# A Fourier mixing block whose loads of the next batch's x are held behind other transfers, and whose sums for the mixing come later

## The chip, the cores and the metric

One NeuronCore of a Trainium2 chip runs the whole program. The metric is device time in microseconds (us), the median of three runs.

## The reference

Two stages on x of shape (8 batches, 3136 positions, 256 channels). The first is a convolution by Fourier transform along the positions; the second adds a two-dimensional transform's real part, normalizes each row, and applies a two-layer product.

```
X = rfft(x, axis=1);  Y = X * (filt_r + 1j*filt_i);  y = irfft(Y, n=3136, axis=1)
mixed = real(fft(fft(y, axis=1), axis=2))
u = y + mixed;  un = (u - mean(u)) / sqrt(var(u) + 1e-6)        # per row of 256
out = u + relu(un @ w_ch1) @ w_ch2                              # 256 -> 1024 -> 256
```

## The kernel before

**Stages of one batch.** The transforms are written as matrix products in two stages each. `forward1` loads x of a batch in seven pieces of 448 KB (`x<-x`), takes the largest magnitude of each piece on VectorE (`absmax`, tile `mx`), makes a scale from all seven (TensorE transposes `pt_x` and spreads `pb_x`), and multiplies by s1 in 14 steps (`s<-x,s`); each step's result goes to DRAM (`d<-ast`). `forward2` loads it back in seven chunks (`at<-d`), multiplies by s2 (`s<-s,at`), applies the filter on VectorE and GpSimd (`yt`), and turns the result by a DMA transpose (`z<-y`). In `fold` GpSimd forms the sums and differences (`ef`, `eo`) that the mixing needs, in a ring of 1920 slots. `inverse1` multiplies z (`i<-z,i`, two products a chunk) and stores to DRAM (`d<-bt`). `inverse2` loads that back in seven pieces of 448 KB (`b<-d`), multiplies by i2 (`y<-b,i`, 14 products a batch) and stores rows to DRAM (`dy<-ys`).

**Groups.** The second part works on 49 groups of 256 slots (6.125 groups a batch). `fetch` loads a group's rows (`y<-dy`); `prepare` mixes (`mix`), normalizes and transposes by DMA (`ut<-u`); `first_product` (`h<-ut,w1s`, 48 matmuls a group) and `second_product` (`acc<-w2s,h`, 96 a group) follow, and `out<-y` stores. Each h is read by ScalarE and then by VectorE (line 746), into two PSUM buffers in turn.

**What sets the order.** Python generators are advanced step by step in the main loop over q, eight q a group: `advance` moves the forward stages (STEPS = 59 steps a batch), `give` the second inverse stage (BACK steps a batch). A scheduler then orders each engine's instructions by its own timeline; `after(key)` puts an instruction behind the marked one on the same engine. The first product of `inverse2` and of `forward2` of a batch stand behind the last h matmul traced. Every DMA is issued from one queue, SP, in order. The pool `xp` has seven buffers of one size for x, at and z together; `b` has two.

Of the kernel before, what the change touches and what calls it, by code (L numbers as in the profile page):

```python
# [25 lines left out]
NS = N // 2  # L26
# [11 lines left out]
BACK = 15  # L38
EARLY = 0.5
RISE = 28  # L40
SOON = 930
LOAD_AT = (15, 16, 17, 18, 19, 27, 28, 25)
# [3 lines left out]
BOUND_AT = (63, 76)  # L46
SPLIT_AT = (63, 101)
# [143 lines left out]
def _program(ctx, tc, nc, a, NB):  # L191
# [166 lines left out]
    def forward1(b, d1):  # L358
# [3 lines left out]
        for q in range(7 + lag):  # L362
            with after(("y", 0), ("un", 0)) if b == 1 else nullcontext():
                if q < 7:
                    nc.sync.dma_start(xs[q], a["x"][b, :, 4 * q : 4 * q + 4])
# [33 lines left out]
    def forward2(b, d1, d2):  # L399
# [108 lines left out]
        for c in range(9):  # L508
            work = [
                (c, spectrum, 0), (c, spectrum, 1), (c, fold, None), (c - 2, inverse1, 0), (c - 2, inverse1, 1),  # L510
# [7 lines left out]
    def inverse2(b, d2):  # L518
# [6 lines left out]
        def load(c):  # L525
            if c < 7:
                bts[c] = fp.tile([112, 4, 2, 256], F16, tag="b2", name=f"b2_{b}_{c}", bufs=2)
                with after("dy"):
                    nc.sync.dma_start(bts[c].rearrange("p j h c -> p (j h) c"), d2v[:, 8 * c : 8 * c + 8])

        def store(k, s, r, ys, c, j0):
            rows = dy[k, 224 * c : 224 * c + 224].rearrange("(j s q) c -> s q j c", j=4, s=2)
            marks["dy"] = nc.sync.dma_start(rows[s, :, j0], ys[r : r + 28, j0]).ins

        load(0)
        yield
# [113 lines left out]
    def prepare(g):  # L650
# [52 lines left out]
        for t, (g0, g1) in enumerate(tiles):  # L703
# [10 lines left out]
            marks["ut", g] = nc.sync.dma_start_transpose(ut[:, t, :, :m], u16[:m].rearrange("p k d l q -> p (k d l q)")).ins  # L714
# [36 lines left out]
    def second_product(g, f):  # L751
# [8 lines left out]
        for t, (g0, g1) in enumerate(tiles):  # L760
# [12 lines left out]
            if f == 7:  # L773
# [3 lines left out]
                marks["out", g] = nc.sync.dma_start(a["out"][:, g0:g1].rearrange("k s c -> s k c"), y[:m, t]).ins  # L777
# [96 lines left out]
    def give(n):  # L874

        while come[0] < min(n, NB * BACK) and done[0] >= STEPS * (come[0] // BACK + 1):
# [59 lines left out]
    for q in range(8 * ng + LAG):  # L936
# [70 lines left out]
```

## Time and profile before

| what | value |
|---|---|
| median of 3 runs | 1554.77 us (1550.2 to 1554.8) |
| the profiled execution | 1556.41 us |
| its span, first to last instruction | 1554.6 us |
| granted TensorE clock over the span | 0.942 |

The clock is a share of full speed: 1.00 is 2.4 GHz, 0.50 is 1.2 GHz. A row of a timeline begins with the start and the length in us; what stands in brackets at its end is the engine's idle time just before it and what ended it.

### The profile page before, as it was taken

The numbers are of one execution on the slowest core, as the hardware profiler recorded it, in microseconds if no ns is written. First come the engines' busy times: TensorE is split into PE (matmuls) and PEld (weight loads), VectorE is DVE, ScalarE is ACT, GpSimd is POOL, SyncE is SP. The second block draws the span as 40 slices with busy tenths as digits, with TensorE's granted clock in tenths as the row PEclk, the third lists the DMA queues.
The fourth block names the chain that finished last, engine by engine and source line by source line (L and its number), as shares of the span: only waits on it lengthen the run. The fifth ranks groups of instructions, "written<-read, shape, count | busy, mean of one in ns | idle before, by whom it ended". The sixth has DMA issues, their size and how long they took to land.

```text
span 1554.6 us, 30100 instructions
## 1 busy us (share of the span) xinstructions
PE 1403.4 (90%) x11203; PEld 939.8 (60%) x11203; DVE 1097.4 (71%) x2395; ACT 758.4 (49%) x1409; POOL 537.3 (35%) x675
## 2 busy tenths in 40 slices
PE   5354997889999999899999999999998989999998
PEld 1341665546666577566675666666675666766666
DVE  5884876687757878687857877688766877564553
ACT  3354445274645555264544654365643645543432
POOL 3661048305720185005640086005730076201100
PEclk8555998989999999999999999999999999999999
DMA  8979269768993798648984698839984598645521
GB/s 287 264 182 263 61 169 204 188 177 177 233 232 90 198 223 204 165 122 190 220 202 136 183 219 197 215 96 218 218 215 127 160 209 189 162 104 114 124 52 41
DMA packets 446386, 273.16 MB, mean 176 GB/s; under 512 B 235520, under 2 KB 412720, under 8 KB 446240
## 3 DMA queue, kind: packets, MB, share of 16 engines
q1 hardware_dynamic: 446240, 271.25, 71.1%
q8 instruction: 88, 1.44, 0.4%
q14 instruction: 58, 0.48, 0.1%
HBM read 113.36 MB, written 102.76 MB: 139 GB/s over the span
## 4 chain that ended last, share of the span: by engine, by line
PE 66%; DMA 15%; DVE 9%; issue 5%; ACT 2%; POOL 2%; SPq 1%; DVEq 0%; ACTq 0%; POOLq 0%
PE h L736 26%; PE acc L765 25%; PE y L549 3%; DMA at<-d 3%; PE s L386 3%; DMA b<-d 3%; DMA d<-bt 2%; DMA d<-ast 2%; PE mix L618 2%; DMA x<-x 2%; DVE y L628 1%; PE i L495 1%; PE i L496 1%; PE i L497 1%; PE s L434 1%
## 5 line engine op out<-in xcount | busy, mean ns | idle before, releaser
L736 PE MATMUL h<-ut,w1s 128*128 128x512 f16 x2352 | 590.2, 385 | 20.8 <-DMA ut<-u 15.0
L765 PE MATMUL acc<-w2s,h 128*128 128x256 f16 x4704 | 599.8, 274 | 1.7 <-DVE y L774 1.6
L765 PEld LDWEIGHTS <-h 128*128 128x128 f16 x4704 | 457.0, 98 | 140.6 <-issue 15.3
L746 DVE SCALAR_TENSOR_TENSOR h<-h,h 128x512 f16<-128x512 f32 x392 | 267.7, 684 | 253.6 <-ACT h L745 252.5
L745 ACT ACTIVATE h<-h 128x512 f16<-128x512 f32 x392 | 233.1, 595 | 394.3 <-PE h L736 387.4
L736 PEld LDWEIGHTS <-w1s 128*128 128x128 f16 x2352 | 223.3, 99 | 246.8 <-issue 44.4
L713 POOL TENSOR_TENSOR u<-un,u 128x512 f16<-128x512 f32 x94 | 107.7, 1160 | 712.3 <-ACT u L711 681.5
L628 DVE SCALAR_TENSOR_TENSOR y<-mix,alpha,y 128x508 f32<-128x508 f32 (+1 forms) x368 | 156.0, 474 | 13.7 <-PE mix L618 10.0
L556 ACT ACTIVATE ys<-y,alpha 128x512 f32<-128x512 f32 x112 | 76.5, 686 | 97.7 <-PE y L549 94.7
L448 POOL TENSOR_TENSOR yt<-yt,t 128x224 f32<-128x224 f32 x105 | 69.3, 660 | 151.6 <-DVE t L444 86.0
L454 POOL TENSOR_TENSOR y<-yt,y 128x448 f16<-128x448 f32 x105 | 110.0, 1050 | 20.7 <-ACT y L453 19.3
L708 ACT ACTIVATE un<-y,sb 128x256 f32<-128x256 f32 x196 | 101.6, 590 | 29.2 <-DVE sb L701 27.0
L549 PE MATMUL y<-b,i 112*64 112x512 f16 (+1 forms) x480 | 76.7, 409 | 41.9 <-DMA b<-d 41.7
L500 DVE TENSOR_TENSOR bt<-i,bt 112x512 f16<-112x512 f32 x112 | 75.9, 683 | 44.0 <-ACT bt L499 43.8
L440 DVE SCALAR_TENSOR_TENSOR yt<-s,pF,ft 128x448 f32<-128x448 f32 x112 | 75.6, 675 | 34.9 <-PE s L435 30.6
L499 ACT CAST bt<-i 112x512 f16<-112x512 f32 x112 | 64.7, 582 | 63.6 <-PE i L497 45.8
L453 ACT CAST y<-yt 128x448 f16<-128x448 f32 x112 | 62.8, 562 | 66.7 <-POOL yt L449 60.8
L434 PE MATMUL s<-s,at 112*128 112x56 f16 x896 | 67.2, 194 | 28.2 <-DMA at<-d 23.8
L386 PE MATMUL s<-x,s 112*112 112x512 f16 x294 | 87.3, 390 | 2.8 <-ACT x L380 1.2
L774 DVE SCALAR_TENSOR_TENSOR y<-acc,beta,y 128x512 f32<-128x512 f32 x98 | 71.7, 741 | 19.4 <-PE acc L765 18.7
L495 PE MATMUL i<-z,i 112*112 112x256 f16 x224 | 65.6, 293 | 19.6 <-DMA z<-y 14.2
L389 DVE TENSOR_TENSOR ast<-s,ast 112x512 f16<-112x512 f32 x98 | 66.4, 680 | 22.4 <-ACT ast L388 22.2
(127 smaller groups left out, 1652.1 us busy)
## 6 DMA issues: line engine op xcount, KB each, us to landing
x<-x SPq DMA_DIRECT2D x56, 448.0 KB
d<-ast SPq DMA_DIRECT2D x112, 224.0 KB
at<-d SPq DMA_DIRECT2D x56, 448.0 KB
d<-bt SPq DMA_DIRECT2D x112, 224.0 KB
b<-d SPq DMA_DIRECT2D x56, 448.0 KB
out<-y SPq DMA_DIRECT2D x98, 256.0 KB
y<-dy SPq DMA_DIRECT2D x92, 256.0 KB
dy<-ys SPq DMA_DIRECT2D x208, 112.0 KB
```

The lines of the kernel that those rows point to most:

```text
L386: nc.tensor.matmul(p, s1[:, hs], x16[:, hx], start=i == 0, stop=i == 2)
L434: nc.tensor.matmul(o, w, s2[:, U, 0].rearrange("p (r k) -> p r k", r=2), start=True, stop=False)
L454: last = half(b, hf == 1).tensor_tensor(ylo, ytv, yhi, op=ALU.subtract)
L495: nc.tensor.matmul(p[:, i], i1[:, j + i, 0], z[:, i, 0], start=True, stop=False)
L549: nc.tensor.matmul(p[64 * h : 64 * h + 64, js], i2[:, t, h, i], bt[:, o + js.start : o + js.stop, h], start=i == 0, stop=i == 1,)
L628: nc.vector.scalar_tensor_tensor(out, p, al, y, op0=ALU.mult, op1=ALU.add)
L708: nc.scalar.activation(un[:m, k], y[:m, t, k], AF.Identity, bias=sb[:m, i, 1:2], scale=sb[:m, i, 3:4])
L713: marks["u16", g] = low.tensor_tensor(u16[:m, :, :, 1], unv, u16[:m, :, :, 0], op=ALU.subtract).ins
L736: marks["pe"] = nc.tensor.matmul(p[:, c0 : c0 + n].rearrange("p (t k q) -> p t k q", k=2, q=m), w1s[:, d, hw, 128 * f : 128 * f + 128], ut ...
L745: nc.scalar.activation(h[:, 0, :nt], p[:, :nt], AF.Relu)
L746: marks["h"] = nc.vector.scalar_tensor_tensor(h[:, 1, :nt], p[:, :nt], 0.0, h[:, 0, :nt], op0=ALU.max, op1=ALU.subtract).ins
L765: nc.tensor.matmul(acc[:m, k], h[:, hh, c0 : c0 + m], w2s[:, f, hw], start=f == 0 and k == 0 and i == 0, stop=f == 7 and k == 1 and i == 2,)
```

## The change

`inverse2` gets two more idle steps between its first load and its first product (WAIT = 2), so a batch has 17 steps of it in place of 15; `give` may begin one step before a batch's forward stages end, at most one step for each q, and runs ahead by `soon`. A batch's forward stages may not begin before the first step of the second inverse stage of the batch before (the load `b_0`) is traced. Each x load stands behind the latest traced transfer among `ut<-u`, `out<-y`, `b<-d` and `dy<-ys` (mark "sp"). `fold` of a chunk is traced one chunk later, behind the products of `inverse1`. EARLY goes from 0.5 to 0.56; two places for the weights move along by the two steps.

```
@@ -35,16 +35,18 @@
 
 PAUSE = 2
 STEPS = 22 + PAUSE + 7 * 5
-BACK = 15
-EARLY = 0.5
+WAIT = 2
+BACK = 1 + WAIT + 14
+EARLY = 0.56
 RISE = 28
 SOON = 930
+LOADED = 300
 LOAD_AT = (15, 16, 17, 18, 19, 27, 28, 25)
 LOAD_AFTER = (6, 7, 8, 9, 10, None, None, None)
 LOAD_IN = ("ys", "ys", "ys", "ut", "ut", "ys", "ys", "ys")
 WIDEN_AT = (22, 22, 28, 52, 53, 54, 55, 55)
-BOUND_AT = (63, 76)
-SPLIT_AT = (63, 101)
+BOUND_AT = (65, 78)
+SPLIT_AT = (65, 103)
 FILTERS_AT = (2, 0, 1, 4, 6, 3, 8, 5)
 FILTERS_ON_ACT = (0, 3, 4, 6)
 
@@ -362,7 +364,8 @@
         for q in range(7 + lag):
             with after(("y", 0), ("un", 0)) if b == 1 else nullcontext():
                 if q < 7:
-                    nc.sync.dma_start(xs[q], a["x"][b, :, 4 * q : 4 * q + 4])
+                    with after("sp"):
+                        nc.sync.dma_start(xs[q], a["x"][b, :, 4 * q : 4 * q + 4])
                 if q >= lag:
                     with after("h"):
                         absmax(m[:, q - lag : q - lag + 1], xs[q - lag], AX.XY)
@@ -507,7 +510,8 @@
             yield
         for c in range(9):
             work = [
-                (c, spectrum, 0), (c, spectrum, 1), (c, fold, None), (c - 2, inverse1, 0), (c - 2, inverse1, 1),
+                (c, spectrum, 0), (c, spectrum, 1), (c - 2, inverse1, 0), (c - 2, inverse1, 1),
+                (c - 1 if c < 7 else c - 2 if c == 8 else -1, fold, None),
             ]
             for ch, f, arg in work:
                 if 0 <= ch < 7:
@@ -526,14 +530,17 @@
             if c < 7:
                 bts[c] = fp.tile([112, 4, 2, 256], F16, tag="b2", name=f"b2_{b}_{c}", bufs=2)
                 with after("dy"):
-                    nc.sync.dma_start(bts[c].rearrange("p j h c -> p (j h) c"), d2v[:, 8 * c : 8 * c + 8])
+                    marks["sp"] = nc.sync.dma_start(
+                        bts[c].rearrange("p j h c -> p (j h) c"), d2v[:, 8 * c : 8 * c + 8]
+                    ).ins
 
         def store(k, s, r, ys, c, j0):
             rows = dy[k, 224 * c : 224 * c + 224].rearrange("(j s q) c -> s q j c", j=4, s=2)
-            marks["dy"] = nc.sync.dma_start(rows[s, :, j0], ys[r : r + 28, j0]).ins
+            marks["sp"] = marks["dy"] = nc.sync.dma_start(rows[s, :, j0], ys[r : r + 28, j0]).ins
 
         load(0)
-        yield
+        for _ in range(1 + WAIT):
+            yield
         for c in range(14):
             if c % 2 == 0:
                 load(c // 2 + 1)
@@ -711,7 +718,7 @@
             nc.scalar.copy(u16[:m, :, :, 0], unv)
             low = nc.vector if g < 2 else nc.gpsimd
             marks["u16", g] = low.tensor_tensor(u16[:m, :, :, 1], unv, u16[:m, :, :, 0], op=ALU.subtract).ins
-            marks["ut", g] = nc.sync.dma_start_transpose(ut[:, t, :, :m], u16[:m].rearrange("p k d l q -> p (k d l q)")).ins
+            marks["sp"] = marks["ut", g] = nc.sync.dma_start_transpose(ut[:, t, :, :m], u16[:m].rearrange("p k d l q -> p (k d l q)")).ins
             yield
         ready[g] = (y, ut)
 
@@ -774,7 +781,7 @@
                 nc.vector.scalar_tensor_tensor(
                     y[:m, t], acc[:m], beta[:m], y[:m, t], op0=ALU.mult, op1=ALU.add
                 )
-                marks["out", g] = nc.sync.dma_start(a["out"][:, g0:g1].rearrange("k s c -> s k c"), y[:m, t]).ins
+                marks["sp"] = marks["out", g] = nc.sync.dma_start(a["out"][:, g0:g1].rearrange("k s c -> s k c"), y[:m, t]).ins
 
     def widen(dst, raw, name):
 
@@ -866,6 +873,8 @@
 
         while done[0] < min(n, NB * STEPS):
             b, s = divmod(done[0], STEPS)
+            if s == 0 and come[0] < BACK * (b - 1) + 1:
+                return
             if s in folds and b * NS + folds[s] - RING > mixed[0]:
                 return
             next(forth)
@@ -873,18 +882,22 @@
 
     def give(n):
 
-        while come[0] < min(n, NB * BACK) and done[0] >= STEPS * (come[0] // BACK + 1):
+        while come[0] < min(n, NB * BACK) and done[0] >= STEPS * (come[0] // BACK + 1) - 1:
             next(home)
             come[0] += 1
 
-    folds = {20 + PAUSE + max(4 + 3 * ch, 5 * ch): 224 * ch + 224 for ch in range(7)}
+    folds = {22 + PAUSE + (4, 9, 14, 19, 24, 29, 34)[ch]: 224 * ch + 224 for ch in range(7)}
 
     def need(slot):
 
-        return BACK * (slot // NS) + 2 * (slot % NS // 224) + 3
+        return BACK * (slot // NS) + 1 + WAIT + 2 + 2 * (slot % NS // 224)
+
+    def soon(slot):
+
+        return max(need(slot), BACK * ((slot + LOADED) // NS) + 1 + WAIT)
 
     def bring(slot):
-        advance(STEPS * (slot // NS + 1))
+        advance(STEPS * (slot // NS + 1) - 1)
         give(need(slot))
         assert come[0] >= need(slot)
 
@@ -945,8 +958,8 @@
         next(work, None)
         if q >= LAG:
             second_product(*divmod(q - LAG, 8))
+        give(min(come[0] + 1, soon(32 * q + SOON)))
         advance(int(STEPS * (1 + min((q + 1) / RISE, (q + 1) / per + EARLY))))
-        give(BACK * (32 * q + SOON) // NS)
         if f == 0 and g + 2 < ng:
             bring(groups[g + 2][-1][1] - 1)
             fetch(g + 2)
```

The line numbers of the change lie 3 to 7 above those of before. In the names, `d_5` is the DRAM tensor of batch 5, `bt_6_1` the second product of its last chunk 6, `b_5_0` the first load of its second inverse stage; `x_0` to `x_6` are then of batch 6. A number at a name's end only counts tiles.

On SP, before, from the end of the first inverse stage of batch 5:

```order
L501 DMA d_5_10101<-bt_4_0_12426 112x1024
L501 DMA d_5_10101<-bt_4_1_12437 112x1024
L714 DMA_TRANSPOSE ut_12231<-u_28_0_12309 128x8x128
L714 DMA_TRANSPOSE ut_12231<-u_28_1_12342 128x8x128
L365 DMA x_5_12525<-x 112x1024
L501 DMA d_5_10101<-bt_5_0_12448 112x1024
L501 DMA d_5_10101<-bt_5_1_12459 112x1024
L501 DMA d_5_10101<-bt_6_0_12470 112x1024
L365 DMA x_6_12526<-x 112x1024
L501 DMA d_5_10101<-bt_6_1_12481 112x1024
L529 DMA b_5_0_12486<-d_5_10101 112x8x256
L529 DMA b_5_1_12599<-d_5_10101 112x8x256
```

The same place in the change:

```order
L504 DMA d_5_10129<-bt_5_0_12260 112x1024
L504 DMA d_5_10129<-bt_5_1_12306 112x1024
L504 DMA d_5_10129<-bt_6_0_12317 112x1024
L504 DMA d_5_10129<-bt_6_1_12355 112x1024
L533 DMA b_5_0_12396<-d_5_10129 112x8x256
L784 DMA out<-y_11128 128x2x256 x2
L533 DMA b_5_1_12482<-d_5_10129 112x8x256
L368 DMA x_0_12503<-x 112x1024
L368 DMA x_1_12504<-x 112x1024
L368 DMA x_2_12505<-x 112x1024
L368 DMA x_3_12506<-x 112x1024
```

Before, the x loads stand among the stores `d<-bt` (`x_0` to `x_4` further up), ahead of `b_5_0`; in the change all seven stand behind it, and here behind `b_5_1` too.

On SP in the change, at the end of batch 4, from the stores of the first second-stage tile `ys_0` on (before, all seven x loads stood ahead of `bt_6_0` here):

```order
L539 DMA dy_9972<-ys_0_10066 28x3x256
L539 DMA dy_9972<-ys_0_10066 28x4x256
L539 DMA dy_9972<-ys_0_10066 28x3x256
L368 DMA x_0_10130<-x 112x1024
L368 DMA x_1_10131<-x 112x1024
L368 DMA x_2_10132<-x 112x1024
L368 DMA x_3_10133<-x 112x1024
L368 DMA x_4_10134<-x 112x1024
L368 DMA x_5_10135<-x 112x1024
L533 DMA b_4_2_10208<-d_4_7593 112x8x256
L368 DMA x_6_10136<-x 112x1024
```

All x loads of batch 5 stand behind the stores of `ys_0`, which need the second product `y_1` of batch 4.

On TensorE, at the start of `forward2` of batch 2, where `s_2_0_0` is the first product that reads `at`; before:

```order
L765 MATMUL acc_1_3608<-w2s,h_5_7_3830 128x256
L765 LDWEIGHTS h_5_7_3830
L765 MATMUL acc_1_3608<-w2s,h_5_7_3830 128x256
L765 LDWEIGHTS h_5_7_3830
L765 MATMUL acc_1_3608<-w2s,h_5_7_3830 128x256
L434 LDWEIGHTS at_0_3658
L434 MATMUL s_2_0_0_3726<-s_83,at_0_3658 128x2x28
```

In the change:

```order
L389 LDWEIGHTS s_81
L389 MATMUL s_2_13_3530<-x_2_13_3527,s_81 112x512
L556 LDWEIGHTS i_85
L556 MATMUL y_7_3651<-b_1_3_3285,i_85 64x512
L556 LDWEIGHTS i_85
L556 MATMUL y_7_3651<-b_1_3_3285,i_85 64x512
L556 LDWEIGHTS i_85
L556 MATMUL y_7_3651<-b_1_3_3285,i_85 64x512
L556 LDWEIGHTS i_85
L556 MATMUL y_7_3651<-b_1_3_3285,i_85 64x512
L437 LDWEIGHTS at_0_3569
L437 MATMUL s_2_0_0_3662<-s_83,at_0_3569 128x2x28
```

Before, 24 h, 50 acc and 16 mix matmuls stand between the last product of `forward1` (`s_2_13`) and `s_2_0_0`; in the change only the four of `y_7`.

## Rows read from the trace of the kernel before

**Rows 1.** The page's first part: busy us, share of the span, instructions.

```profile
PE 1403.4 (90%) x11203; PEld 939.8 (60%) x11203; DVE 1097.4 (71%) x2395; ACT 758.4 (49%) x1409; POOL 537.3 (35%) x675
```

**Rows 2.** Waits of TensorE: us in total, times, longest.

```profile
PE y L549 <- DMA b<-d: 41.7, 11, 6.1
PE s L434 <- DMA at<-d: 23.8, 12, 7.6
PE h L736 <- DMA ut<-u: 15.0, 4, 6.0
```

**Rows 3.** Timeline of TensorE, first products of inverse2, batches 2 to 6.

```profile
461.90 0.73 PE L549 MATMUL y<-b,i 112*64 112x256 f16 x8 [2.23 <-DMA b<-d]
...
640.55 1.06 PE L549 MATMUL y<-b,i 112*64 112x256 f16 x8 [6.15 <-DMA b<-d]
641.55 2.74 PE L736 MATMUL h<-ut,w1s 128*128 128x512 f16 x6
...
826.60 1.08 PE L549 MATMUL y<-b,i 112*64 112x256 f16 x12 [3.74 <-DMA b<-d]
...
998.70 1.06 PE L549 MATMUL y<-b,i 112*64 112x256 f16 x8 [3.52 <-DMA b<-d]
...
1173.70 1.92 PE L549 MATMUL y<-b,i 112*64 112x256 f16 x12 [5.33 <-DMA b<-d]
```

**Rows 4.** Windows behind these waits: us, PE, PEld, DVE, ACT, POOL, PEclk, DMA, GB/s.

```profile
462.30:465.70 3.40, 3.40 (x20) 2.11 (x16) 0.00 (x0) 0.69 (x1) 0.00 (x0) 0.50 1.35 133
639.80:646.60 6.80, 6.05 (x26) 3.30 (x26) 1.65 (x3) 1.28 (x2) 0.00 (x0) 0.50 0.08 20
827.50:830.90 3.40, 3.40 (x12) 1.45 (x11) 1.54 (x5) 1.54 (x3) 0.00 (x0) 0.50 0.35 90
998.20:1005.00 6.80, 6.30 (x26) 2.83 (x26) 1.65 (x6) 1.97 (x3) 0.00 (x0) 0.50 0.49 114
1172.30:1179.10 6.80, 5.40 (x23) 2.68 (x23) 0.00 (x0) 1.97 (x3) 0.00 (x0) 0.50 0.63 160
```

**Rows 5.** Timeline of TensorE in batch 7, from inverse1's last product to inverse2's first.

```profile
1341.28 0.27 PE L497 MATMUL i<-z,i 112*112 112x256 f16 x1
1341.39 1.46 PE L736 MATMUL h<-ut,w1s 128*128 128x512 f16 x6
1342.68 1.47 PE L765 MATMUL acc<-w2s,h 128*128 128x256 f16 x12
1343.99 1.46 PE L736 MATMUL h<-ut,w1s 128*128 128x512 f16 x6
...
1350.59 1.06 PE L549 MATMUL y<-b,i 112*64 112x256 f16 x12
```

**Rows 6.** Chain that ended last, batches 0 and 5: start us, us, what.

```profile
104.15 2.23 DMA d<-bt
...
988.95 5.53 DMA d<-bt
994.55 4.11 DMA b<-d
```

**Rows 7.** Timeline of SP in batch 1: issue of x for batch 2.

```profile
282.82 3.02 SPq L365 DMA_DIRECT2D x<-x  x6
```

**Rows 8.** Timeline of VectorE: the first and the last of seven absmax of batch 2.

```profile
288.29 1.22 DVE L261 TENSOR_REDUCE mx<-x 112x1 f32<-112x1024 f32 x1 [2.83 <-DMA x<-x]
...
299.56 1.22 DVE L261 TENSOR_REDUCE mx<-x 112x1 f32<-112x1024 f32 x1 [0.92 <-DMA x<-x]
```

**Rows 9.** Timeline of TensorE, waits from batch 1 to 2, and at batch 4.

```profile
295.64 2.72 PE L736 MATMUL h<-ut,w1s 128*128 128x512 f16 x6 [2.97 <-DVE h L746]
...
313.51 0.55 PE L257 MATMUL pb_x<-row_x,ones 1*128 1x2 f32 x2 [4.97 <-DVE mv L686]
...
361.46 0.20 PE L434 MATMUL s<-s,at 112*128 112x56 f16 x1 [1.21 <-DMA at<-d]
...
715.74 0.23 PE L434 MATMUL s<-s,at 112*128 112x56 f16 x1 [3.39 <-DMA at<-d]
```

More of the change, by code (lines that the diff above doesn't have):

```diff
@@ L37 @@
 STEPS = 22 + PAUSE + 7 * 5
-BACK = 15
-EARLY = 0.5
+WAIT = 2
+BACK = 1 + WAIT + 14
+EARLY = 0.56
 RISE = 28
 SOON = 930
+LOADED = 300
 LOAD_AT = (15, 16, 17, 18, 19, 27, 28, 25)
@@ L364, in forward1 @@
                 if q < 7:
-                    nc.sync.dma_start(xs[q], a["x"][b, :, 4 * q : 4 * q + 4])
+                    with after("sp"):
+                        nc.sync.dma_start(xs[q], a["x"][b, :, 4 * q : 4 * q + 4])
                 if q >= lag:
@@ L509, in forward2 @@
             work = [
-                (c, spectrum, 0), (c, spectrum, 1), (c, fold, None), (c - 2, inverse1, 0), (c - 2, inverse1, 1),
+                (c, spectrum, 0), (c, spectrum, 1), (c - 2, inverse1, 0), (c - 2, inverse1, 1),
+                (c - 1 if c < 7 else c - 2 if c == 8 else -1, fold, None),
             ]
@@ L528, in load @@
                 with after("dy"):
-                    nc.sync.dma_start(bts[c].rearrange("p j h c -> p (j h) c"), d2v[:, 8 * c : 8 * c + 8])
+                    marks["sp"] = nc.sync.dma_start(
+                        bts[c].rearrange("p j h c -> p (j h) c"), d2v[:, 8 * c : 8 * c + 8]
+                    ).ins
         def store(k, s, r, ys, c, j0):
             rows = dy[k, 224 * c : 224 * c + 224].rearrange("(j s q) c -> s q j c", j=4, s=2)
-            marks["dy"] = nc.sync.dma_start(rows[s, :, j0], ys[r : r + 28, j0]).ins
+            marks["sp"] = marks["dy"] = nc.sync.dma_start(rows[s, :, j0], ys[r : r + 28, j0]).ins
         load(0)
-        yield
+        for _ in range(1 + WAIT):
+            yield
         for c in range(14):
@@ L868, in advance @@
             b, s = divmod(done[0], STEPS)
+            if s == 0 and come[0] < BACK * (b - 1) + 1:
+                return
             if s in folds and b * NS + folds[s] - RING > mixed[0]:
@@ L874, in give, with soon @@
     def give(n):
-        while come[0] < min(n, NB * BACK) and done[0] >= STEPS * (come[0] // BACK + 1):
+        while come[0] < min(n, NB * BACK) and done[0] >= STEPS * (come[0] // BACK + 1) - 1:
             next(home)
             come[0] += 1
-    folds = {20 + PAUSE + max(4 + 3 * ch, 5 * ch): 224 * ch + 224 for ch in range(7)}
+    folds = {22 + PAUSE + (4, 9, 14, 19, 24, 29, 34)[ch]: 224 * ch + 224 for ch in range(7)}
     def need(slot):
-        return BACK * (slot // NS) + 2 * (slot % NS // 224) + 3
+        return BACK * (slot // NS) + 1 + WAIT + 2 + 2 * (slot % NS // 224)
+    def soon(slot):
+        return max(need(slot), BACK * ((slot + LOADED) // NS) + 1 + WAIT)
     def bring(slot):
-        advance(STEPS * (slot // NS + 1))
+        advance(STEPS * (slot // NS + 1) - 1)
         give(need(slot))
@@ L947, in _program @@
             second_product(*divmod(q - LAG, 8))
+        give(min(come[0] + 1, soon(32 * q + SOON)))
         advance(int(STEPS * (1 + min((q + 1) / RISE, (q + 1) / per + EARLY))))
-        give(BACK * (32 * q + SOON) // NS)
         if f == 0 and g + 2 < ng:
```

8 lines of the change are left out of this document (4 added, 4 removed).

## The prediction

> **What bounds the kernel now.** I read the busy times first, then who TensorE waits for, then each of its longer waits on the timeline with the granted clock behind it. TensorE is busy 1403.4 of 1554.6 us, the next engine 1097.4 [rows 1]: time is saved only where TensorE stands idle or runs at the lower clock. Its largest wait is the one this change is about, 41.7 us for the load `b<-d` in front of the first products of `inverse2`; the load `at<-d` follows with 23.8 us and `ut<-u` with 15.0 us [rows 2].
>
> The waits for `b<-d` in batches 2 to 6 are 2.23, 6.15, 3.74, 3.52 and 5.33 us, 21.0 in sum [rows 3]. Each has a tail: behind it the granted clock is 0.50, which is 1.2 GHz in place of 2.4, after TensorE had stood still; six h matmuls then take 2.74 us [rows 3], against 1.46 at the full clock [rows 5]. TensorE is busy 3.40, 6.05, 3.40, 6.30 and 5.40 us in these stretches, 24.6 in sum [rows 4], and the same work at the full clock takes half. So these five waits cost 21.0 + 12.3 = 33.3 us.
>
> Batch 7 is the control that the kernel itself holds: no x of a ninth batch is loaded there. Between the last product of `inverse1` and the first of `inverse2` it has 24 h and 36 acc matmuls, from 1341.55 (1341.28 + 0.27) to 1350.59, 9.0 us, and no wait [rows 5]. Batches 2 to 6 have about as much work in between (18 to 24 h, 36 to 48 acc by the order) and wait. The chain shows why: the last store `d<-bt` takes 2.23 us in batch 0, with no x near, but 5.53 in batch 5, and the load behind it 4.11 [rows 6]. The x loads stand in the same queue just ahead of it, and seven of them are not quick: in batch 1 they are issued from 282.82 on [rows 7], the first is there at 288.29 and the last at 299.56 [rows 8], so 5.5 us for the first and (299.56 - 288.29) / 6 = 1.9 us for each more.
>
> **The change part by part.** No product, copy or byte is added or removed; what changes is places, and each step that moves takes its DMAs along on SP.
>
> *`b_0` ahead of x, and two idle steps.* By the order of the change, 24 h + 36 acc stand in front of the first product in batches 3 and 4, just as in batch 7 before, and 24 h + 48 acc or more in batches 2, 5 and 6. Six h take 1.29 us from start to start and twelve acc 1.31 [rows 5], so this is 9.1 to 11 us against a chain that needs at most 9.0 without x. The 33.3 us should go, but not whole: in batches 3 and 4 there is no margin, and in batch 6 a fetch and a transposing load still stand ahead of `b_6_0`. The bounds are nothing gained (if x was not the cause) and 33.3; I leave 5 and take **-28**.
>
> *x of the next batch comes later.* Places below are us after the last product of `inverse1`, counted off the order with the prices of h and acc just given. Behind x wait `absmax` on VectorE, and behind that, in VectorE's order, the second reader of h, which frees its PSUM buffer. That this reaches TensorE is seen in batch 1: `absmax` waits 2.83 us for x [rows 8], and TensorE then 2.97 us for VectorE [rows 9]. In batches 2, 3, 5 and 6 four loads go out right behind `b_0` or `b_1`, and the rest behind the stores of `ys_0`: counted with 1.9 us a load they land about 27 to 29 us after the last product of `inverse1`, and the scale's product `pt_x` stands 33 to 34 us after it; the last `absmax` stands 25 to 28 us after it, so VectorE is held for a few us, which the two PSUM buffers (two f-steps of 2.6 us each, by the 1.29 and 1.31 above) cover: nothing. In batch 4 all seven stand behind those stores. `y_1` stands 14.4 us after the last product; with its copy and six stores the first issue comes at about 18.5, the first x lands at 18.5 + 5.5 = 24, and six more and `b_4_2` at 1.9 each bring the last to 37. VectorE's order has it at 28.4 and is free again at about 38.4; TensorE gets 5.2 us beyond 28.4 and waits some 5 us, with a slow stretch like those of [rows 4], about 2.5 us. **+7.5**; bounds nothing and, in all five batches, 37.5.
>
> *Batch 1 to 2.* Here the order of TensorE changes most. `y_0` of batch 1 has only 18 h, 16 acc and 16 mix matmuls (6.5 us) in front of it: a wait of about 2.5. x for batch 2 stands behind `b_1_0`, and `x_6` behind `b_1_1`, so it lands some 10 us later (two casts, 2.23 for the store, about 4 for `b_1_0` [rows 6] and 1.9 for `b_1_1` lie ahead of it now), and `pt_x` stands at 20.0 us: a wait of about 6. And `s_2_0_0` has four matmuls of 0.2 us in front of it where the load `at` needs about as long as before: then 11.5 us of work covered all but 1.21 us [rows 9], so some 10 us stay open now. In the other direction the waits of 2.97, 4.97 and 1.21 us go from these places [rows 9]. 18.5 - 9.2 = **+9**; bounds 0 (the scheduler put nothing else there because nothing else was ready, so the time may be lost before as well) and 15, with slow clock behind.
>
> *`at` in batches 3 and 4.* In front of the first `at` product of batch 4 stood 12 h and 31 acc, 7 us of work with mix and y, and a wait of 3.39 us [rows 9]; now 20 h and 45 acc, 11 us. With the slow stretch behind it and a little from batch 3, **-6.5**, bounds -2 and -8.
>
> *Prologue.* Of the 41.7 us [rows 2] 20.7 lie outside batches 2 to 6, nearly all of it in batch 0, where x of batch 1 is loaded between the loads `b_0_3` to `b_0_6`. Those now come first; but `inverse2` there also waits for its own stores, and the first group's transpose now stands behind `b_0_6` and two x. Bounds 0 and -10, **-3**.
>
> *The sums moved back.* GpSimd does the same work; before the last z of a batch stand as many sums as before, but the eo of one chunk. The mixing products wait for nothing in the trace of before, and forward stages end half a group earlier. Nothing. EARLY and the places of the weights move work, not its amount: nothing.
>
> Sum: 1556.4 of the profiled execution - 28 + 7.5 + 9 - 6.5 - 3 = 1535.4; the median of the runs is 1.6 us below that execution, so 1533.8. I say **1534**.
>
> **A rule against it.** In batch 1 x is issued from 282.82 on [rows 7], and VectorE waits for its first piece from 285.46 (288.29 - 2.83) on [rows 8]: even now x is hardly early. The Trainium skill, "DMA: Bandwidth & Descriptors", section "Rules for kernel authors", says to issue a DMA early and wait for it late so that its fixed cost overlaps with compute; holding x back is the opposite. By that rule the time is the first rival's. The trace bears it out for a load that is needed within some 15 us, and not for `b<-d`, which is hurt by what is issued early ahead of it.
>
> **The rivals.** *Held x is late in every batch (slower).* The price of batch 4 in all five: 1533.8 + 4 x 7.5 = 1564. It decides from the point where the last x lands more than some 5 us behind the last `absmax`'s place, 25 to 28 us after the last `inverse1` product. For it: the wait of 2.97 us through VectorE; against it: four of seven loads go out early there, and seven took 16.7 us from issue to landing. *x was not what delayed `b<-d`.* Then half of the 28 stays, 1548, or with the loss from batch 1 to 2 sized at its bound of 15, 1554: no change. For it: x is not all that stands ahead of the store and the load on SP (fetches and transposes do too); against it: batch 7. *The losses don't come.* No 7.5, and from batch 1 to 2 nothing: 1517. For it: TensorE may only wait at another place for the same thing; against it: the four matmuls in front of `s_2_0_0`.
>
> **How the numbers follow.** The forecast (1520 to 1547) has 0.55, the losses that don't come 0.15 (1508 to 1520), x that was not the cause 0.15 (1547 to 1558), held x late everywhere 0.13 (1558 to 1570), the rest 0.02. Up to 0.3% (4.7 us) a measurement can't tell from no change. Faster by more: 0.55 + 0.15 + 0.06 of the third case = 0.76; within: 0.10; slower: 0.14. The range 1510 to 1558 leaves out the slower rival and the lowest end.
>
> **What would show it.** Right: no wait, or under 1 us, in front of the first `y<-b` product of batches 2 to 6, no 0.50 stretch behind it, `d<-bt` near 2.3 us; a wait of some 10 us for `at<-d` at the start of `forward2` of batch 2; a wait of some 5 us for VectorE or `pt_x` about 35 us after the last `inverse1` product of batch 4. Wrong: waits for `b<-d` of 3 us and more; `mx` waiting for x in each batch and TensorE for `h` behind it; or new waits for `ut<-u`, which the order can't show.

## The result, and the profile after

The changed kernel is slower: 1565.52 us against 1550.2 us for the kernel before on the same chip, ratio 1.0064 (95% interval 1.0038 to 1.009). The forecast was 1534 us and faster. The profiled execution of the changed kernel took 1565.74 us, its span is 1563.9 us, the mean granted clock 0.951. The kernel before moved from 1550 to 1555 us between the measurements below, so everything is compared by ratios to it. The ratios are those on record, from the fast runs of both kernels, and not quotients of the two medians (here 1.0099). Where two ratios are compared, their difference is given in per cent of the kernel before. A profile is one execution, and executions of one kernel differ by several us (of the change 1559.7 to 1566.2), so a few us between two traces alone decide nothing.

The page's first part, and the waits of TensorE (us in total, times, longest), of the changed kernel:

```profile
PE 1395.1 (89%) x11203; PEld 928.9 (59%) x11203; DVE 1095.3 (70%) x2395; ACT 757.3 (48%) x1409; POOL 537.8 (34%) x675
```

```profile
PE s L437 <- DMA at<-d: 27.3, 13, 9.6
PE h L743 <- DMA ut<-u: 24.5, 13, 6.7
PE y L556 <- DMA b<-d: 24.2, 10, 4.4
PE h L743 <- DVE h L753: 18.0, 14, 3.3
```

TensorE is busy 8.3 us less than in [rows 1], because less of its work runs at the lower clock, and yet the span is 9.3 us longer: it stands idle 17.6 us more. The wait for `b<-d` has fallen from 41.7 us [rows 2] to 24.2; `ut<-u` has risen from 15.0 to 24.5, and two waits for VectorE have grown, for `h` from 5.8 to 18.0 and for `y` from 1.6 to 5.0.

Where the time lies is read from windows. First the kernel before, cut into four stretches (us, PE, PEld, DVE, ACT, POOL, PEclk, DMA, GB/s):

```profile
0.00:149.00 149.00, 66.38 (x437) 42.64 (x438) 101.10 (x213) 65.43 (x127) 67.60 (x85) 0.62 0.95 250
149.00:285.00 136.00, 124.56 (x1020) 84.85 (x1020) 100.50 (x203) 68.51 (x128) 58.53 (x77) 0.95 0.63 148
285.00:366.00 81.00, 64.80 (x455) 39.74 (x453) 63.00 (x143) 37.02 (x67) 6.83 (x8) 0.90 0.73 194
366.00:1554.60 1188.60, 1147.65 (x9296) 772.58 (x9293) 832.75 (x1838) 587.42 (x1087) 404.30 (x507) 0.98 0.70 168
```

Then the changed kernel, cut at about the same points of its program:

```profile
0.00:149.00 149.00, 65.61 (x437) 42.01 (x438) 99.53 (x210) 65.33 (x127) 67.85 (x85) 0.64 0.90 237
149.00:290.00 141.00, 120.33 (x977) 79.72 (x976) 100.42 (x202) 65.90 (x123) 55.57 (x74) 0.93 0.62 150
290.00:386.00 96.00, 77.91 (x588) 49.01 (x589) 70.21 (x154) 44.13 (x80) 19.50 (x25) 0.91 0.81 203
386.00:1563.90 1177.90, 1131.27 (x9204) 758.17 (x9202) 825.14 (x1833) 581.94 (x1079) 394.86 (x493) 1.00 0.70 167
```

Both begin with 437 matmuls in 149 us, so in these two executions the prologue gave nothing. The stretches do not hold the same work, and the matmuls in them are counted by kind. The last stretch is 10.7 us shorter and has 92 matmuls fewer in it: 48 of `s<-s,at`, 27 acc, 9 h and 8 y. At the full clock these follow each other by 0.026, 0.109, 0.216 and 0.139 us in the trace of before, together 7.2 us. So the steady batches gained 3.5 us, and 12.8 are lost before 386 us. Of these, 12.3 lie between 149 and 290 us, in batch 1: the stretch is 5 us longer and has 24 h and 19 acc fewer in it, 7.3 us. The passage from batch 1 to 2 behind it lost 0.5 us.

Inside the steady stretch two things nearly cancel. Idle TensorE there is 1188.60 - 1147.65 = 41.0 us before and 46.6 after, and the waits of the two windows say why. Before:

```profile
PE y L549 <- DMA b<-d: 21.0, 5, 6.1
PE s L434 <- DMA at<-d: 12.1, 7, 3.4
PE h L736 <- DVE h L746: 1.7, 3, 1.2
PE acc L765 <- DVE y L774: 1.6, 2, 1.2
```

After:

```profile
PE h L743 <- DVE h L753: 14.4, 12, 3.3
PE s L437 <- DMA at<-d: 8.1, 9, 1.7
PE h L743 <- DMA ut<-u: 8.0, 7, 2.4
PE y L556 <- DMA b<-d: 5.7, 4, 2.0
PE acc L772 <- DVE y L781: 5.0, 4, 3.2
```

The loads fell by 15.3 (`b`) and 4.0 us (`at`), and the clock in this stretch rose from 0.98 to 1.00: busy time fell by 16.4 us, 9.2 more than the missing matmuls explain. VectorE took 16.1 us back and `ut` 8.0.

The place that answers to [rows 3] and [rows 4] is now clean in batches 3 and 4: in batch 4 the first product of `inverse2` waits for nothing and runs at the full clock, in batch 3 it waits 1.69 us in place of 6.15 (timeline of TensorE, then windows behind the products):

```profile
641.05 1.06 PE L556 MATMUL y<-b,i 112*64 112x256 f16 x12 [1.69 <-DMA b<-d]
...
815.77 0.52 PE L556 MATMUL y<-b,i 112*64 112x256 f16 x6
```

```profile
641.00:648.00 7.00, 6.95 (x60) 4.81 (x60) 2.34 (x3) 3.33 (x7) 2.31 (x2) 1.00 1.10 283
815.00:822.00 7.00, 7.00 (x59) 4.30 (x58) 2.07 (x3) 3.47 (x7) 3.05 (x3) 1.00 0.76 189
```

Where the time went instead is read from three engines in batch 3, whose last `inverse1` product ends at 630.2 us. On SP, two of the seven x loads (`x_4`, `x_5`) go out only at 653.16, behind the stores `dy<-ys` and two transposes:

```profile
640.21 1.57 SPq L368 DMA_DIRECT2D x<-x  x3
...
648.79 2.83 SPq L721 DMA_TRANSPOSE ut<-u  x1
651.67 1.44 SPq L539 DMA_DIRECT2D dy<-ys  x3
653.16 1.84 SPq L368 DMA_DIRECT2D x<-x  x2
```

VectorE stands in `absmax` for x, 3.59 us for the second piece and 5.28 for `x_4`, and h comes after it:

```profile
647.57 1.22 DVE L263 TENSOR_REDUCE mx<-x 112x1 f32<-112x1024 f32 x1 [3.59 <-DMA x<-x]
...
658.30 1.22 DVE L263 TENSOR_REDUCE mx<-x 112x1 f32<-112x1024 f32 x1 [5.28 <-DMA x<-x]
659.44 0.68 DVE L753 SCALAR_TENSOR_TENSOR h<-h,h 128x512 f16<-128x512 f32 x1
```

TensorE, at its next two groups of h:

```profile
660.17 1.46 PE L743 MATMUL h<-ut,w1s 128*128 128x512 f16 x6 [1.04 <-DVE h L753]
...
665.50 1.46 PE L743 MATMUL h<-ut,w1s 128*128 128x512 f16 x6 [2.12 <-DVE h L753]
```

The largest loss of this kind lies in batch 5. There two transposes `ut<-u` hold the queue for 10.26 us behind four x loads and two loads `y<-dy`, the last three x go out only behind them, and TensorE waits twice for VectorE (SP, then TensorE):

```profile
988.19 2.84 SPq L368 DMA_DIRECT2D x<-x  x4
...
992.32 10.26 SPq L721 DMA_TRANSPOSE ut<-u  x2
```

```profile
1013.99 1.46 PE L743 MATMUL h<-ut,w1s 128*128 128x512 f16 x6 [3.32 <-DVE h L753]
1018.66 1.42 PE L772 MATMUL acc<-w2s,h 128*128 128x256 f16 x8 [3.21 <-DVE y L781]
1019.87 2.77 PE L743 MATMUL h<-ut,w1s 128*128 128x512 f16 x6
```

Over the program, VectorE's wait for x has gone from 11.9 us to 51.9 (waits of VectorE, before and after; batch 0 has 7.5 of the 11.9 and 8.5 of the 51.9):

```profile
DVE mx L261 <- DMA x<-x: 11.9, 10, 4.9
```

```profile
DVE mx L263 <- DMA x<-x: 51.9, 34, 5.3
```

And at the start of `forward2` of batch 2, where [rows 9] had 1.21 us:

```profile
370.18 0.23 PE L437 MATMUL s<-s,at 112*128 112x56 f16 x1 [9.63 <-DMA at<-d]
```

### The profile page after: what moved, and what is told of

Its sections match the earlier page's. It is cut to its first block, busy times and chain, and to the rows that moved or that the text cites. A ratio compares the mean times of both kernels' runs of the same rounds, so it can differ in the third digit from the quotient of the medians.

```text
span 1563.9 us, 30055 instructions
## 1 busy us (share of the span) xinstructions
PE 1395.1 (89%) x11203; PEld 928.9 (59%) x11203; DVE 1095.3 (70%) x2395; ACT 757.3 (48%) x1409; POOL 537.8 (34%) x675
## 4 chain that ended last, share of the span: by engine, by line
PE 58%; DMA 16%; DVE 9%; issue 5%; POOL 5%; ACT 4%; SPq 3%; DVEq 0%; ACTq 0%; POOLq 0%
PE h L743 23%; PE acc L772 22%; DMA x<-x 4%; PE s L389 3%; DMA ut<-u 3%; PE y L556 3%; DMA at<-d 2%; DMA d<-ast 2%; DMA z<-y 2%; DVE y L635 2%; PE mix L625 1%; DMA b<-d 1%; PE i L498 1%; DVE mx L263 1%; PE i L499 1%
## 5 line engine op out<-in xcount | busy, mean ns | idle before, releaser
L743 PE MATMUL h<-ut,w1s 128*128 128x512 f16 x2352 | 589.8, 384 | 42.6 <-DMA ut<-u 24.5
L772 PEld LDWEIGHTS <-h 128*128 128x128 f16 x4704 | 454.6, 98 | 151.9 <-issue 17.6
L263 DVE TENSOR_REDUCE mx<-x 112x1 f32<-112x1024 f32 x56 | 68.1, 1217 | 52.0 <-DMA x<-x 51.9
L556 PE MATMUL y<-b,i 112*64 112x512 f16 (+1 forms) x480 | 75.4, 400 | 24.2 <-DMA b<-d 24.2
L437 PE MATMUL s<-s,at 112*128 112x56 f16 x896 | 63.7, 194 | 34.8 <-DMA at<-d 27.3
L498 PE MATMUL i<-z,i 112*112 112x256 f16 x224 | 65.8, 294 | 25.4 <-DMA z<-y 15.6
L437 PEld LDWEIGHTS <-at 112*128 112x128 f16 x896 | 57.8, 100 | 40.7 <-DMA at<-d 33.0
```

The lines of the kernel that those rows point to most:

```text
L263: nc.vector.tensor_reduce(dst, src, axis=axis, op=ALU.max, apply_absolute_value=True)
L437: nc.tensor.matmul(o, w, s2[:, U, 0].rearrange("p (r k) -> p r k", r=2), start=True, stop=False)
L556: nc.tensor.matmul(p[64 * h : 64 * h + 64, js], i2[:, t, h, i], bt[:, o + js.start : o + js.stop, h], start=i == 0, stop=i == 1,)
L743: marks["pe"] = nc.tensor.matmul(p[:, c0 : c0 + n].rearrange("p (t k q) -> p t k q", k=2, q=m), w1s[:, d, hw, 128 * f : 128 * f + 128], ut ...
L772: nc.tensor.matmul(acc[:m, k], h[:, hh, c0 : c0 + m], w2s[:, f, hw], start=f == 0 and k == 0 and i == 0, stop=f == 7 and k == 1 and i == 2,)
```

## The experiments

**The theories.** A: the x loads, held behind other transfers, come too late for `absmax`; VectorE stands there, h and y behind it are late, and TensorE pays what it gained at `b<-d`. B: the hold is harmless, and another part of the change loses the time (the sums moved back, the idle steps, EARLY, the gate on the next batch), by the order it gives batch 1 and the prologue.

### Absmax that does not wait for x

`absmax` of batches 1 to 7 reads a stretch of the filters of the same size, so their scale comes from the filters and not from x. All transfers stay.

```
-    absmax(m[:, q - lag : q - lag + 1], xs[q - lag], AX.XY)
+    absmax(m[:, q - lag : q - lag + 1], ft[:112, 0, 0, :1024])
```

In the changed kernel:

> The changed kernel, where the seven absmax of each batch from batch 1 on read a piece of the filters of the same size instead of x (so the scale is that of the filters; the work on VectorE stays). The order of the loads stays that of the change. Theory A (x held back comes late, VectorE stands in its absmax, and TensorE waits for h behind it): the waits of TensorE for h and y on VectorE fall from 23 us to under 8, and the kernel is 10 to 18 us faster than the changed one, about 1550. Theory B (the loss comes from the moved sums and the new order from batch 1 to 2, not from x): within 4 us of the changed kernel.

Measured: 1543.0 us, ratio 0.9919 (0.9891 to 0.9947), 1.45% below the changed kernel and more than the 10 to 18 us of theory A. TensorE's waits for VectorE's h and y fall from 23.0 to 3.9 us. The instruction itself costs the same from either source, 1209 ns at the mean against 1217.

The same edit in the kernel before is the control:

> The same edit in the kernel before: the control. VectorE waited for x there only in batch 1 (some 4 us) and TensorE some 3 us behind it. Both theories: within 5 us of the kernel before.

Measured: 1559.38 us, ratio 1.0035 (1.0015 to 1.0054). Where x was early, nothing is gained; the time is 0.35% longer, just outside the 5 us. That is the direction of A. But this edit also lets the scheduler place `absmax` and what follows elsewhere, so not all of the 1.45% need be the wait; the last run under "x earlier, absmax later" gains 1.26% by it in a kernel where VectorE hardly waits for x.

The same in the changed kernel for batches 3 to 7 alone (`if b > 2`):

> The changed kernel, with absmax reading the filters in place of x for batches 3 to 7 only (their scale comes from the filters then); batches 1 and 2 are as in the change. Theory A, with the loss in every batch: most of the 22 us of the run with absmax elsewhere come back, 1545 to 1554. If the loss lies from batch 1 to 2 (and in their order): 1556 to 1566.

Measured: 1546.24 us, ratio 0.9968 (0.9944 to 0.9992). By the ratios some 0.96% of the 1.45% comes back from batches 3 to 7, the rest from batches 1 and 2.

### Parts of the change undone

x not held; the order then puts it ahead of `b_0` again:

```
-                    with after("sp"):
-                        nc.sync.dma_start(xs[q], a["x"][b, :, 4 * q : 4 * q + 4])
+                    nc.sync.dma_start(xs[q], a["x"][b, :, 4 * q : 4 * q + 4])
```

> The changed kernel without the hold on x (the x loads need not stand behind the latest transfer any more); by the order, x stands among the stores of the first inverse stage again, ahead of the load b_0, in all batches. The two idle steps, the moved sums and EARLY stay. Theory A: VectorE's waits for x and TensorE's 23 us behind VectorE fall to under 8 us, but the waits for b come back to 10 to 20 us with half clock behind: 1555 to 1570, near the changed kernel. Theory B: the waits for b come back and nothing is won: 1575 to 1590.

Measured: 1558.16 us, ratio 1.0017 (0.9995 to 1.0039). VectorE waits 9.0 us for x, and TensorE again for `b`:

```profile
PE y L555 <- DMA b<-d: 37.2, 12, 8.2
```

This is the range of theory A. The hold buys the wait for `b` and pays with VectorE's; by the ratios it costs 0.47% more than it brings, with intervals that just touch. Without it the change is still no faster than the kernel before.

No idle steps (`WAIT = 0`, `BOUND_AT` and `SPLIT_AT` as before; the hold stays):

> The changed kernel without the two idle steps (WAIT = 0, and the places of the weights as before); x is held. The prediction put the gain of 28 us down to b_0 ahead of x and the two idle steps together. If the hold alone carries it: waits for b<-d of 24 to 30 us, time within 5 us of the change. If the idle steps carry a part: waits for b<-d of 32 us and more, 1568 to 1580.

Measured: 1570.14 us, ratio 1.0118 (1.0086 to 1.0151). Waits of TensorE:

```profile
PE s L437 <- DMA at<-d: 32.1, 11, 13.8
PE y L556 <- DMA b<-d: 27.3, 12, 3.7
```

The wait for `b` is only 3.1 us above the change's, so the hold carries most of that gain, as the first case said. The time is some 8 us above the change, not within 5: the wait for `at` is 4.8 us longer, which neither case had.

The sums in their old place in the change (this edit also lets `give` begin only when a batch's forward stages have ended, as before), and the sums moved back alone in the kernel before:

```
-                (c, spectrum, 0), (c, spectrum, 1), (c - 2, inverse1, 0), (c - 2, inverse1, 1),
-                (c - 1 if c < 7 else c - 2 if c == 8 else -1, fold, None),
+                (c, spectrum, 0), (c, spectrum, 1), (c, fold, None), (c - 2, inverse1, 0), (c - 2, inverse1, 1),
```

> The changed kernel with the sums for the mixing at their old place, ahead of the products of the first inverse stage. Theory A: within 5 us of the changed kernel, unless the order of the x loads moves with it (in batches 4 and 5 x stands earlier here, which theory A makes a gain of some 5 us). Theory B: 8 us or more faster than the changed kernel, most of it before 390 us.

> The kernel before with one part of the change alone: fold of a chunk traced behind the products of inverse1, one chunk later, and the table of its steps. Theory A: the sums cost nothing, 1549 to 1557. Rival: the sums moved back are what lengthens the stretch from 149 to 290 us by some 10 us in the change (waits for ut and z there), then 1558 to 1566.

Measured: 1566.3 us, ratio 1.0073 (1.0045 to 1.0102), for the first, which is the change's time; 1564.63 us, ratio 1.008 (1.005 to 1.0109), for the second, with a wait for `z<-y` of 26.5 us against 14.2 in the kernel before (in an execution of 1573 us, above the median). The second is what the rival of its text expected. In the order of the kernel before the sums moved back cost 0.8%; in that of the change, undoing them gives nothing. They are not why the change is slower, but "nothing" is no rule for them, and by what path they delay z there stays open.

EARLY at 0.5:

> The changed kernel with EARLY at 0.5 again, one part of the change undone; the hold on x stays. Theory A: forward stages of a batch begin no earlier relative to x, so x stays late, 1560 to 1568. Theory B (EARLY is what lengthens the stretch from 149 to 290 us): TensorE loses 15 us there as before, not 26, and the time is 1552 to 1560.

Measured: 1560.72 us, ratio 1.0073 (1.0049 to 1.0098): by the ratios no change. Of theory B no single part that was undone gives the time back. The gate on the next batch and the new pace of `give` (`soon`, one step for each q) were not undone by themselves; that rival stays untested.

The traces show where each run loses its time. The table gives an estimate for each: the time between two points less that of its matmuls, each priced at its start-to-start time at the full clock in the trace of before (an h 0.216 us, an acc 0.109). The points are the first h of groups 0, 4 and 7, and the end; `x_6` stands for the kernel of the next section with `x_6` ahead of `b_2`.

| us lost | before | change | x not held | sums in old place | no idle steps | EARLY 0.5 | `x_6` | `x_6`, EARLY 0.5 |
|---|---|---|---|---|---|---|---|---|
| group 0 to 4 | 18 | 31 | 26 | 26 | 29 | 30 | 30 | 30 |
| group 4 to 7 | 25 | 27 | 28 | 30 | 32 | 20 | 29 | 18 |
| group 7 to end | 73 | 67 | 66 | 69 | 72 | 68 | 59 | 54 |

The loss in batch 1, from group 0 to 4, is there without the hold too and in every run that undoes a part, so theory A explains a part of it at most; the cause of the rest stays open. EARLY at 0.5 loses less from group 4 to 7 in both pairs, but the execution traced in the change was 3.5 us faster than its median, and the ratios show no gain there.

### x earlier, absmax later

x behind the loads `b<-d` alone (the stores, transposes and outputs no longer set the mark):

```
-            marks["sp"] = marks["dy"] = nc.sync.dma_start(rows[s, :, j0], ys[r : r + 28, j0]).ins
+            marks["dy"] = nc.sync.dma_start(rows[s, :, j0], ys[r : r + 28, j0]).ins
```

and the same for `ut<-u` and `out<-y`.

> The changed kernel, with x held behind the loads b<-d alone, not behind the stores dy<-ys, ut<-u and out<-y as well. By the order all of x of a batch then goes out right behind b_0 or b_1 in place of being spread over some 16 to 20 us. Theory A (late x keeps VectorE standing in absmax, and TensorE then waits for h and y): VectorE's waits for x fall from 43 us to under 20, TensorE's waits for VectorE's h fall from 18 to under 8, and the time is 1545 to 1556, no slower than before. Theory B (the loss lies in the order of the prologue and batch 1, which the two idle steps, the gate on the next batch and EARLY set): 1560 to 1567. A third outcome, that x right behind b_1 now delays b_2 and the stores: waits for b<-d above 35 us.

Measured: 1577.93 us, ratio 1.0146 (1.0119 to 1.0173): a miss, and the most telling one. Its trace shows two prices. In batch 4 six x loads are early, but `x_6` is traced behind `b_2` and goes out 17 us after them, behind two transposes that hold the queue for 8.79 us (SP, VectorE, TensorE):

```profile
824.89 2.37 SPq L368 DMA_DIRECT2D x<-x  x2
828.83 8.79 SPq L721 DMA_TRANSPOSE ut<-u  x2
...
842.03 0.60 SPq L368 DMA_DIRECT2D x<-x  x1
```

```profile
848.30 1.22 DVE L263 TENSOR_REDUCE mx<-x 112x1 f32<-112x1024 f32 x1 [6.13 <-DMA x<-x]
```

```profile
851.08 2.33 PE L743 MATMUL h<-ut,w1s 128*128 128x512 f16 x6 [4.55 <-DVE h L753]
```

One load 6.13 us late for VectorE is 4.55 us of TensorE. The second price is in the prologue, where all seven x now stand ahead of the first transposes `ut<-u`: TensorE waits 16.25 us there, against 6.74 in the change.

```profile
156.60 5.30 PE L743 MATMUL h<-ut,w1s 128*128 128x512 f16 x12 [16.25 <-DMA ut<-u]
```

In the change, two more steps between the x loads and `absmax` (61 steps a batch, lag 4; the tables of the weights two steps on):

```
-STEPS = 22 + PAUSE + 7 * 5
+MORE = 2
+STEPS = 22 + PAUSE + MORE + 7 * 5
...
-        lag = 2 if b else 0
+        lag = 2 + MORE if b else 0
...
-            if q < 7:
+            if q < 7 + MORE:
                 yield
```

> The changed kernel, with two more steps of the forward stages between the x loads and absmax (61 steps a batch in place of 59, lag 4 in place of 2); x is held as in the change. By the order the first absmax of a batch stand one or two h later on VectorE, the last ones one h or none, and nothing else moves much. Theory A: VectorE's waits for x fall from 43 us to some 25 and the time to 1550 to 1561. Theory B: 1562 to 1568, as in the change.

Measured: 1563.11 us, ratio 1.0046 (1.0028 to 1.0065); this is theory B's range. VectorE's wait for x falls from 51.9 to 27.5 us, the time hardly. With 59 steps, and the first `absmax` moved towards the last (two in step 5, two in 6, three in 7):

> The changed kernel with 59 steps, the same order of the loads, and only the place of the first absmax of a batch moved: two in step 5, two in step 6, three in step 7 in place of one a step from step 2 on. By the order the first two stand two h later on VectorE, the last one where it was. Theory A (VectorE stands in absmax before x is there): VectorE's waits for x fall from 43 us to 20 to 30, since the last pieces are as late as before, and the time to 1552 to 1562. Theory B (the order of batch 1 and the prologue): 1562 to 1568.

Measured: 1571.39 us, ratio 1.0138 (1.0108 to 1.0168), a miss. VectorE's wait for x fell from 51.9 to 32.8 us with batch 0's, but the last pieces are as late as before, and the three `absmax` that now stand together with their waits make one long hold:

```profile
1027.40 1.86 PE L773 MATMUL acc<-w2s,h 128*128 128x256 f16 x8 [6.34 <-DVE y L782]
```

TensorE's waits for VectorE's h and y are 22.5 us, as in the change (23.0), although VectorE waits 19 us less. My reading is that what counts is how long VectorE is away from h and y in one piece, not the sum of its waits. Why this run is slower than the change is not shown.

Both, x behind `b<-d` alone and `absmax` two steps later:

> Both of the other two: x behind b<-d alone, and absmax two steps later. Theory A: almost no wait of VectorE for x is left, TensorE keeps what b_0 ahead of x gives, and the time is 1538 to 1550, below before. Theory B: 1558 or more, since the prologue and batch 1 are left as in the change.

Measured: 1553.21 us, ratio 0.999 (0.9973 to 1.0007), between the two theories: the 1.46% that x behind `b<-d` alone lost are gone, but nothing is won. Then with x of batch 1 held behind all transfers as in the change, to mend the prologue:

> As the run with x behind b<-d alone and absmax two steps later, but x of batch 1 is held behind all later transfers as in the change. In the two runs with x behind b<-d alone TensorE waits 15 to 16 us for the first ut<-u, which stands behind seven x loads, against 6.7 us in the change. Theory A with that reading: the wait is 6 to 8 us again, the other waits stay, and the time is 1543 to 1549, below before. If the long wait for ut had another cause: 1551 to 1556.

Measured: 1558.0 us, ratio 1.0048 (1.0028 to 1.0067), a miss: the prologue is mended, the first h starting 9.4 us earlier than in the run before this one, but the first h of group 6 9.7 us later: more is lost from batch 1 to 2 than the prologue gave. Last, in that kernel, `x_6` in the step of `x_5`, so ahead of `b_2`:

```
-                if q < 7:
+                for i in (5, 6) if q == 5 else (q,) if q < 5 else ():
```

> As the run with batch 1 held and the rest behind b<-d alone, with the seventh load of x in the step of the sixth, so that by the order it stands ahead of b_2 in place of behind it (with absmax at its old place VectorE waited 4.5 to 6.4 us for just this piece in batches 2 to 4). Theory A: the last waits of VectorE for x in batches 2 to 6 go, and the time is 1540 to 1548, 0 to 4 us below that run. If b_2 and the stores behind x then come late: waits for b<-d of 3 us more, and the time is the same.

Measured: 1553.53 us, ratio 1.0011 (0.9993 to 1.0029), above the 1540 to 1548 expected. In batches 2 to 6 VectorE no longer waits for x; the 16.6 us left are for x of batches 0 to 2:

```profile
DVE mx L264 <- DMA x<-x: 16.6, 13, 4.3
```

From 386 us on TensorE waits 3.8 us for VectorE's h and y, against 19.4 in the change. That is 15.6 us of waits less for 0.53%, some 8 us; the estimates of the table put the 8 us from group 7 on, and where the other half went is not shown. With the whole computation kept, this is the most direct price of late x here, though x and `absmax` both moved.

With `absmax` reading the filters in this kernel:

> The run with x6 ahead of b_2, with absmax reading the filters in place of x in batches 1 to 7. VectorE waits for x there only some 8 us in all any more. Theory A in its plain form (the wait is the price): at most 8 us are to be had, 1545 to 1553. If the remaining 10 us to the run with absmax elsewhere is another order of the same work: no gain, 1550 to 1556. Under 1545: absmax holds VectorE at a bad place even where x is there.

Measured: 1534.39 us, ratio 0.9885 (0.985 to 0.9921), 1.26% less, from which only some 8 us of VectorE's waits could be had. It is the third case of the text. This edit changes the order too, and its price is not that of the wait alone; so the 1.45% of the first experiment do not measure the wait either.

### A version that beats both

The kernel with `x_6` ahead of `b_2`, with EARLY at 0.5:

> The run with x6 ahead of b_2, with EARLY at 0.5. With EARLY undone alone the change gained some 5 us, with 18 in place of 23 us lost from batch 1 to 2. If this adds up: 1545 to 1551, below before. If it is scatter of the order: 1550 to 1560.

Measured: 1539.29 us, ratio 0.9919 (0.9892 to 0.9947): 0.8% below the kernel before and 1.4% below the change, with the whole computation. The window of its last stretch, from about the same point of the program:

```profile
376.00:1537.00 1161.00, 1134.03 (x9242) 764.78 (x9240) 828.08 (x1836) 580.30 (x1077) 403.28 (x505) 0.99 0.71 171
```

TensorE is idle 27.0 us there; it was 41.0 before and 46.6 in the change. By the estimates of the table above, 12 of the 17 us between this trace and the one with EARLY at 0.56 lie from group 4 to 7, most of it ahead of this stretch.

## Why the prediction was wrong

The profiled execution took 1565.74 us where the sum gave 1535.4, 30.3 more. In the steady stretch -28 + 7.5 - 6.5 = -27 were forecast, and -3.5 came: `b` -15.3, `at` -4.0, the clock -9.2, VectorE +16.1, `ut` +8.0, other waits +0.9. At the start -3 + 9 = +6 were forecast, and +12.8 came.

**The step that failed** is the one on x in batches 2, 3, 5 and 6: "VectorE is held for a few us, which the two PSUM buffers ... cover: nothing". TensorE's waits for VectorE in the steady stretch are 14.4 + 5.0 = 19.4 us, and only 1.58 + 2.08 + 0.46 + 0.69 = 4.8 of them lie in batch 4, behind late x in the order I had counted. Of the others 3.5 lie in batch 3, 7.1 in batch 5 and 3.2 in batch 6, which were put at nothing; in batch 2, with 0.7 and none of it near `absmax`, the step held. Two things were wrong in the count. The pieces behind the stores of `ys_0` were to land 27 to 29 us after the last `inverse1` product; the last `absmax` began 663.63 - 630.2 = 33 us after it in batch 3 and 34 in batch 5, because stores and transposes on SP took time that I had given to x alone (10.26 us for two transposes in batch 5). And the cover of 5 us was taken for one wait, where seven `absmax` of 1.22 us and their waits come in a row, so that the next wait may begin before the two buffers are ahead again; that is my reading. In batch 4 that stretch leaves VectorE almost no free time, 15.29 of 16.00 us busy after 2 us of waits for x, and TensorE is busy 11.19 (window):

```profile
830.00:846.00 16.00, 11.19 (x74) 6.61 (x72) 15.29 (x29) 3.08 (x5) 0.00 (x0) 1.00 1.00 263
```

**Batch 1, not in the sum:** the second step that failed. From 149 to 290 us 12.3 us are lost where the prediction had no term (the sums and EARLY stood at nothing). Without the hold 26 of the 31 us of the table are still lost there (18 before), so by these traces the hold is some 5 of the 13 at most; what the rest is stays open.

**b_0 ahead of x: right in direction and nearly in size.** The wait in batches 2 to 6 fell from 21.0 to 4.1 us, with 1.6 new in batch 7. With all that the clock gave, 15.3 + 9.2 = 24.5 us at most came of the 28. It is not quite clean: in batch 2 a later product waits 2.04 us, and six h behind it take 2.77.

**x late in batch 4, +7.5:** 4.8 measured, the wait of 5 us without the slow stretch behind it: the clock stayed at 1.00.

**at, -6.5:** -4.0 (12.1 to 8.1), without its share of the clock. **Prologue, -3:** nothing in the two traces, but they can't decide it: the first h begins at 149.0, 152.5 and 153.8 us in the kernel before and its two variants, and at 145.4 to 148.8 in the twelve traces that hold x of batch 1 as the change does.

**Batch 1 to 2, +9:** +0.5 from 290 to 386 us. The wait of 9.63 us for `at` was the one foreseen (some 10); the wait for `pt_x` did not come. That the 12.8 us of the whole start lie within the bounds of the two terms is luck, since they were lost ahead of this place.

**ut, not in the sum:** +8.0 in the steady stretch. The text had named it as what the order can't show. Of its three signs of being wrong this one came, and `mx` waiting for x with TensorE behind it.

**The sums and EARLY, "nothing":** true in the order of this change, by the two runs that undo them. In other orders each is worth 0.8 to 0.9%: the sums in the kernel before, EARLY once x is early (1.0011 against 0.9919). In these runs a part that moves no work had no price of its own; its price was that of the order that it met.

**The rivals.** Held x late in every batch gave 1564 us. The number is luck: it asks for 7.5 us in each of five batches, 37.5, and VectorE's waits came to 19.4 us; the rest is 8 of `ut` and the loss in batch 1. The Trainium skill, "DMA: Bandwidth & Descriptors", section "Rules for kernel authors" (issue early, wait late), stood for this rival. The trace agrees with its direction: one x load that went out late cost TensorE 4.55 us. That x was not what delayed `b<-d` falls: without the hold the wait is 37.2 us again.

What stays open: how much of the 1.45% with `absmax` elsewhere is the wait and how much the other order, what loses the time in batch 1, by what path the sums moved back delay z in the kernel before, and why EARLY pays by the ratios only with early x.

## What to carry to other kernels

When a transfer is held back to let another pass, follow its consumer to the engine that it stands on and count everything behind it there in one piece, not wait by wait; here TensorE's waits for VectorE took back 16 of some 24 us. Then move the consumer as well: the loss behind VectorE went only when x went right behind the load that it must not delay, and `absmax` later. And where an order is set by a scheduler, measure the parts together; a part that is worth nothing in one order was worth 0.8% in another.

## What was not expected of the hardware

Two transposing DMAs held the queue far longer where several loads of 448 KB had just gone out ahead of them. All `ut<-u` of the changed kernel on SP (least, median and longest in ns, then the first and last start in us):

```profile
L721 SPq DMA_TRANSPOSE ut<-u x98: 1231/1280/5483, 142.6 to 1527.8; - x98
```

In the prologue, two take 4.10 us of SP behind two x loads in the changed kernel, and 11.54 us behind seven when x is held behind `b<-d` alone:

```profile
142.60 4.10 SPq L721 DMA_TRANSPOSE ut<-u  x2
```

```profile
137.11 3.85 SPq L368 DMA_DIRECT2D x<-x  x7
142.26 11.54 SPq L721 DMA_TRANSPOSE ut<-u  x2
```

The two places shown above, 10.26 us behind four x loads and 8.79 behind six, agree; and two others of the changed kernel, at 367.32 us, take 6.11 behind three loads `at<-d`, with no x near. That the loads are the cause is inferred from these places and was not measured by itself.

Idle time in small pieces did not lower the clock in the window of batch 4 above: TensorE is busy 11.19 of 16.00 us at a granted clock of 1.00, with stops of 1.58, 2.08, 0.46 and 0.69 us. Each of the waits of [rows 3], from 2.23 us on, had 0.50 behind it, but the length of one stop does not decide it. In batch 5 of the change a stop of 3.32 us has six h in 1.46 us behind it, the time at the full clock, and only behind the next stop, of 3.21 us, six h take 2.77 (the three rows above). In batch 2 a stop of 2.04 us was followed by six h in 2.77.
